# A fused attention and FFN kernel: batch 0's values loaded in three pieces, another order of the first FFN units, and two pieces of work moved behind batch 2's keys by values

## The chip, the cores and the metric

The kernel runs on one core of a Trainium2 chip. The metric is the device time of one execution in microseconds (us). The kernel before took 326.3 us (median of 3 runs, 325.94 to 326.5). All runs quoted here were in the same, fast state. A ratio is the mean time of one kernel's fast runs over the mean of the other's of the same rounds, so it is not quite the ratio of the medians beside it. Two or more kernels of one batch ran on the same chip and share the runs of the kernel before, so I compare within a batch first.

A profile comes from one execution. Differences of 0.1 to 1 us are below what one whole execution settles, but the profile prints starts to 0.01 us.

## The reference, cut to what matters

```python
q_p, k_p = phi(q), phi(k)             # relu times cos and relu times sin of the position
kv  = einsum('bhsf,bhsd->bhfd', k_p, v)   # per head: keys by values
z   = k_p.sum(axis=2)                     # taken along as a 65th column of v
x   = (q_p @ kv) / (q_p . z + 1e-6)   # 8 batches of 576 rows, 512 columns
g, val = x @ w_gate, x @ w_val        # FFN, 1536 columns in 12 column tiles
out = (gelu(g) * val) @ w_out         # float32, 4608 x 512
```

The inputs are q, k and v of 8 batches x 8 heads x 576 rows x 64. The attention is linear: after keys by values each row of q costs one small matmul and one division.

## The kernel before

All heavy work is on TensorE (PE). The program fixes the order of instructions on every engine by hand. The FFN works in blocks of 576 or 512 rows. Block 0 needs only batch 0's x. Each later block b carries batch b+1's attention between its units. A unit is a gate (four matmuls, then gelu on ScalarE, ACT) and a value (four matmuls, then a product on VectorE, DVE). There are eight PSUM banks, and each call names the bank it uses. To turn a tile is to transpose it by PE. The numerators of a tile are its small matmuls of q with keys by values, and dummies are matmuls without use that pass PE's time at the start.

```python
def gate(n, jt, c0, w, gb):            # 4 matmuls into bank gb, then gelu on ACT
    ...
    nc.scalar.activation(gel[:, 0:w], ps[:, gb, 0:w], AF.Gelu)
def value(n, jt, c0, w, vb):           # 4 matmuls into bank vb, then the product on DVE
    ...
    nc.vector.tensor_mul(hT..., gel[:, 0:w], ps[:, vb, 0:w])
def numer_mm(b, t, bank, g):           # group g of heads goes to bank + g: a tile uses TWO banks
    ... ps[0:rows, bank + g, ...]
def Y(t, bank):                        # numerators and division of x tile t of batch 0
    ...
def X(t, bank, eng):                   # x tile t turned by PE, copied to xT by eng
    ...
def q_by_pe(b, j, bank, eng):          # q tile j turned by PE, copied to qT by eng
    ...
```

The beginning of block 0 as the kernel before has it (cut):

```python
q_by_pe(0, 3, 6, "s")
gate(0, 2, *A, 5)                      # A: columns 0 to 255
X(2, 0, "v")()
sq(4, 1, "s"), sq(4, 0, "v")           # sine product of q tile 4 on ACT, cosine on DVE
gate(0, 3, *A, 4)
value(0, 2, *A, 7)
Y(3, 0)()
value(0, 3, *A, 2)
q_by_pe(0, 4, 3, "s")
gv_unit(0, 0, 256, 128, 5, 6)
gv_unit(0, 1, 256, 128, 4, 7, (X(3, 0, "s"),))
Y(4, 2)()
gv_unit(0, 0, 384, 128, 5, 1)          # "the unit at column 384"
```

The two later pieces that the change moves: `carry(0)`, a GpSimd (POOL) copy of 64 FFN columns from block 0's buffer to block 1's, and `attn_step(1, 5)`, the numerators and division of batch 1's last x tile (64 rows).

## Time and profile before

| view | value |
|---|---|
| median time, span of the profile | 326.3 us, 324.7 us |
| PE busy | 98% |
| first FFN gate | 16.63 us |
| turn of x tile 1 (four L343 after the first gates) | 17.21 us |
| unit at column 384 (L218) | 24.02 us |
| keys by values of batch 1, of batch 2 (L154) | 48.68, 67.55 us |

In a timeline row the columns are start, duration in us, engine, line, operation, what it writes and reads with shapes, the count of merged instructions and, in brackets, the idle time ahead of it with what ended it. A pipelined stream of four 128x512 matmuls is shown as 1.03 us long, but the next stream starts 0.86 us after it: I read starts, not ends. The lines themselves are in the prediction below.

### The profile page before, as it was taken

How to read it: one execution, taken by the hardware profiler on the slowest of the kernel's cores; microseconds unless marked ns; L12 is line 12 of the kernel's file. 1: busy time of each engine (PE TensorE's matmuls, PEld its weight loads, DVE VectorE, ACT ScalarE, POOL GpSimd, SP SyncE). 2: the span in 40 equal slices, each digit the busy share in tenths (PEclk: the TensorE clock that was granted, in tenths of full speed). 3: DMA queues.
4: the chain of work that ended last, by engine and by line, in shares of the span. 5: the costliest groups of instructions: out<-in, count | busy, mean ns of one | idle time of the engine just before them, and what ended most of it. 6: DMA issues, size and time to landing. Idle time of an engine off the chain costs nothing.

```text
span 324.7 us, 5863 instructions
## 1 busy us (share of the span) xinstructions
PE 317.4 (98%) x2218; PEld 167.3 (52%) x2218; DVE 168.2 (52%) x380; ACT 151.3 (47%) x271; POOL 22.0 (7%) x43
## 2 busy tenths in 40 slices
PE   7999999999999999999999999999999999999994
PEld 2597856455445544544455445544554444444443
DVE  5785776677663575366636574637454222222210
ACT  6574774852583247325642565237522222323321
POOL 2650010000100010001000100010000100100000
PEclk9999999999999999999999999999999999999999
DMA  7999999999999929991999279946433111000124
GB/s 228 284 204 275 232 295 311 333 217 155 299 193 356 206 50 194 324 245 51 191 324 239 55 147 299 302 66 121 107 70 78 32 32 34 32 32 32 37 63 97
DMA packets 88299, 55.56 MB, mean 171 GB/s; under 512 B 53072, under 2 KB 83536, under 8 KB 88272
## 3 DMA queue, kind: packets, MB, share of 16 engines
q1 hardware_dynamic: 81744, 48.84, 60.8%
q0 software_dynamic: 6096, 5.90, 10.2%
q10 hardware_dynamic: 432, 0.46, 0.5%
q8 instruction: 17, 0.28, 0.4%
q14 instruction: 10, 0.08, 0.1%
HBM read 37.75 MB, written 9.44 MB: 145 GB/s over the span
## 4 chain that ended last, share of the span: by engine, by line
PE 94%; DVE 3%; issue 1%; ACT 0%; DVEq 0%
PE ps L218 28%; PE ps L229 28%; PE ps L259 27%; PE ps L154 3%; PE ps L170 3%; PE ps L127 3%; DVE kp L135 1%; PE ps L324 1%; PE ps L277 1%; DVE vx L141 1%; PE ps L343 1%; DVE xb L185 0%; DVE rec L184 0%; ACT xT L346 0%; DVE qp L135 0%
## 5 line engine op out<-in xcount | busy, mean ns | idle before, releaser
L234 DVE TENSOR_TENSOR hT<-gel,ps 128x512 bf16<-128x512 f32 (+5 forms) x126 | 76.2, 608 | 92.1 <-PE ps L229 91.7
L218 PE MATMUL ps<-xT,wg_sb 128*128 128x512 bf16 (+5 forms) x504 | 113.4, 349 | 0.1
L229 PE MATMUL ps<-xT,wv_sb 128*128 128x512 bf16 (+5 forms) x504 | 113.2, 348 | 0.0
L223 ACT ACTIVATE gel<-ps 128x512 f32<-128x512 f32 (+5 forms) x126 | 67.4, 536 | 73.9 <-PE ps L218 48.8
L259 PE MATMUL ps<-wo_sb,hT 128*128 128x512 bf16 x420 | 96.5, 379 | 0.0
L218 PEld LDWEIGHTS <-wg_sb 128*128 128x128 bf16 x504 | 47.1, 98 | 44.5
L229 PEld LDWEIGHTS <-wv_sb 128*128 128x128 bf16 x504 | 45.7, 98 | 39.0
L259 PEld LDWEIGHTS <-hT 128*128 128x128 bf16 x420 | 40.8, 98 | 47.7
L288 ACT COPY o_sb<-ps 128x512 f32<-128x512 f32 x35 | 20.5, 586 | 76.0 <-PE ps L259 75.9
L185 DVE TENSOR_TENSOR xb<-ps,rec 128x512 bf16<-128x512 f32 (+2 forms) x41 | 27.8, 678 | 1.8 <-DMA xr<-xb 0.3
L182 DVE TENSOR_SCALAR den<-ps 128x8 f32<-128x8 f32 (+2 forms) x41 | 6.7, 164 | 41.1 <-PE ps L170 41.0
L137 ACT ACTIVATE kp<-kf,sin_c 128x512 bf16<-128x512 f32 (+1 forms) x41 | 25.4, 681 | 0.3 <-DMA kf<-in_k_dram 0.3
L170 PEld LDWEIGHTS <-qT 128*128 128x128 bf16 (+1 forms) x320 | 15.1, 98 | 8.3 <-issue 0.4
L137 ACT ACTIVATE qp<-qf,sin_c 128x512 bf16<-128x512 f32 x28 | 19.3, 714 | 0.0
L135 DVE TENSOR_SCALAR kp<-kf,cos_c 128x512 bf16<-128x512 f32 (+1 forms) x45 | 18.7, 463 | 0.8 <-DMA kf<-in_k_dram 0.8
L135 DVE TENSOR_SCALAR qp<-qf,cos_c 128x512 bf16<-128x512 f32 x40 | 17.8, 488 | 0.0
L170 PE MATMUL ps<-kv,qT 128*128 128x65 bf16 (+1 forms) x320 | 16.6, 194 | 0.1
L209 POOL COPY xT<-xr 128x256 bf16<-128x256 bf16 x7 | 2.8, 401 | 198.0 <-DMA xr<-xb 198.0
L127 PE MATMUL ps<-hT 128*128 128x512 bf16 x34 | 11.1, 484 | 1.7 <-DVE par_i L104 1.7
L154 PEld LDWEIGHTS <-kp 128*128 128x128 bf16 x320 | 10.8, 97 | 3.2 <-issue 0.9
L154 PE MATMUL ps<-vx,kp 128*128 128x65 bf16 x320 | 11.1, 193 | 0.6 <-DVE vx L141 0.3
L141 ACT CAST vx<-vf 128x1280 bf16<-128x1280 f32 (+1 forms) x9 | 9.7, 1076 | 1.2 <-DMA vf<-in_v_dram 1.2
(54 smaller groups left out, 89.0 us busy)
## 6 DMA issues: line engine op xcount, KB each, us to landing
out_dram<-o_sb SPq DMA_DIRECT2D x38, 128.0 KB, 2.4
kf<-in_k_dram SPq DMA_DIRECT2D x7, 640.0 KB, 7.1
out_dram<-o_sb SPq DMA_DIRECT2D x16, 256.0 KB, 2.8
qf<-in_q_dram SPq DMA_DIRECT2D x6, 640.0 KB, 5.9
vf<-in_v_dram SPq DMA_DIRECT2D x6, 640.0 KB, 8.8
kf<-in_k_dram SPq DMA_DIRECT2D x7, 512.0 KB, 6.0
qf<-in_q_dram SPq DMA_DIRECT2D x6, 512.0 KB, 4.9
vf<-in_v_dram SPq DMA_DIRECT2D x6, 512.0 KB, 7.8
```

Of the source, the lines that this page charges most:

```text
L127: nc.tensor.matmul(ps[:, bank, :], lhsT=junk[:, 0:128], rhs=junk, start=True, stop=True)
L135: nc.vector.tensor_scalar(d, s, col, 0.0, op0=ALU.mult, op1=ALU.max)
L137: nc.scalar.activation(d, s, AF.Relu, scale=col)
L154: nc.tensor.matmul(ps[:, bank, (h % 4) * (D + 1):(h % 4 + 1) * (D + 1)], lhsT=kp[:, j, h, :], rhs=vx[b % 2][:, j, h, 0:D + 1], start=(j == ...
L170: nc.tensor.matmul(ps[0:rows, bank + g, (h % 4) * (D + 1):(h % 4 + 1) * (D + 1)], lhsT=qT[b % 2][:, t, h, 0:rows], rhs=kv[b % 2][:, h, 0:D ...
L185: nc.vector.tensor_tensor(xb[0:rows, g0:g1], nd[:, :, :, 0:D], rec[0:rows, 0:n, :, None].to_broadcast([rows, n, 4, D]), op=ALU.mult,)
L218: nc.tensor.matmul(ps[:, gb, 0:w], lhsT=wg_sb[:, ct, jt * 128:(jt + 1) * 128], rhs=xT[:, ct, p0:p0 + w], start=(ct == 0), stop=(ct == CT - 1),
L223: nc.scalar.activation(gel[:, 0:w], ps[:, gb, 0:w], AF.Gelu)
L229: nc.tensor.matmul(ps[:, vb, 0:w], lhsT=wv_sb[:, ct, jt * 128:(jt + 1) * 128], rhs=xT[:, ct, p0:p0 + w], start=(ct == 0), stop=(ct == CT - 1),
L234: nc.vector.tensor_mul(hT[n % 2][:, jt, 64 + c0:64 + c0 + w], gel[:, 0:w], ps[:, vb, 0:w])
L259: nc.tensor.matmul(ps[:, bank, :], lhsT=hT[n % 2][:, jt, c0:c0 + 128], rhs=wo_sb[:, jt, :], start=(jt == 0), stop=(jt == JT - 1),)
L288: nc.scalar.copy(o_sb, ps[:, bank, :])
```

## The change

Its intent, as far as the code tells: start keys by values of batch 0 earlier by loading the second half of v in two pieces and by giving ACT and DVE other shares of the copies; drop four of the 34 dummy matmuls; put another FFN unit ahead of x tile 3's numerators; and take a POOL copy and a division out of the way of the keys by values of batches 1 and 2.

```diff
-    load(vf, v, 0, 4, 8)
+    load(vf, v, 0, 4, 6)
+    load(vf, v, 0, 6, 8)
 ...
-    kv_half(0, 0, 4, None)
-    q_evac(0, 1, 1, "v")
-    dummies(2)
+    kv_heads(0, 0, 4, 4)
+    q_evac(0, 0, 0, "v")
+    q_evac(0, 1, 1, "s", 0, 4)
     cast_v(0, 4, 6, "v")
-    cast_v(0, 6, 8, "s")
-    kv_evac(0, 0, 4, "v")
-    kv_half(0, 1, 5, "s")
+    cast_v(0, 6, 7, "v")
+    kv_evac(0, 0, 4, "s")
+    cast_v(0, 7, 8, "s")
+    dummies(1)
+    kv_heads(0, 4, 6, 5)
 ...                                    # numerators, second half of kv, q tile 2's turn moved
     q_by_pe(0, 3, 6, "s")
+    X(2, 0, "v")()
     gate(0, 2, *A, 5)
-    X(2, 0, "v")()
+    gate(0, 3, *A, 4)
     sq(4, 1, "s"), sq(4, 0, "v")
-    gate(0, 3, *A, 4)
+    gv_unit(0, 0, 256, 128, 1, 2)
+    Y(3, 0)()
     value(0, 2, *A, 7)
-    Y(3, 0)()
-    value(0, 3, *A, 2)
-    q_by_pe(0, 4, 3, "s")
-    gv_unit(0, 0, 256, 128, 5, 6)
-    gv_unit(0, 1, 256, 128, 4, 7, (X(3, 0, "s"),))
-    Y(4, 2)()
+    value(0, 3, *A, 3)
+    q_by_pe(0, 4, 6, "s")
+    gv_unit(0, 1, 256, 128, 5, 2, (X(3, 0, "s"),))
+    Y(4, 3)()
     gv_unit(0, 0, 384, 128, 5, 1)
 ...                                    # other banks for the units after it
-        (11, 1): (L(carry, 0), ),
 ...
-    mid[1][3].append(L(attn_step, 1, 5))
+    mid[1][5].append(L(attn_step, 1, 5, 4))
+    mid[1][5].append(L(carry, 0))
```

More of the change, by code (lines that the diff above doesn't have):

```diff
@@ L148, in turn_q, with kv_heads @@
         )
-    def kv_half(b, g, bank, eng="s"):
-        for h in range(4 * g, 4 * g + 4):
+    def kv_heads(b, h0, h1, bank):
+        for h in range(h0, h1):
             for j in range(NJ + 1):
@@ L159, in kv_half @@
                 )
-        if eng is not None:
-            kv_evac(b, g, bank, eng)
+    def kv_half(b, g, bank, eng="s"):
+        kv_heads(b, 4 * g, 4 * g + 4, bank)
+        kv_evac(b, g, bank, eng)
     def kv_evac(b, g, bank, eng):
@@ L363 @@
     load_w(4, 8)
-    for j in range(2):
-        sq(j, 0, "v"), sq(j, 1, "s")
-        q_by_pe(0, j, j, None)
-    dummies(3)
-    q_evac(0, 0, 0, "v")
+    sq(0, 0, "v"), sq(1, 1, "s"), sq(0, 1, "v"), sq(1, 0, "v")
+    q_by_pe(0, 0, 0, None)
+    q_by_pe(0, 1, 1, None)
+    dummies(2)
     cast_v(0, 0, 2, "v")
     cast_v(0, 2, 4, "s")
-    kv_half(0, 0, 4, None)
-    q_evac(0, 1, 1, "v")
-    dummies(2)
+    kv_heads(0, 0, 4, 4)
+    q_evac(0, 0, 0, "v")
+    q_evac(0, 1, 1, "s", 0, 4)
     cast_v(0, 4, 6, "v")
-    cast_v(0, 6, 8, "s")
-    kv_evac(0, 0, 4, "v")
-    kv_half(0, 1, 5, "s")
+    cast_v(0, 6, 7, "v")
[3 more added lines that the diff above has]
+    kv_heads(0, 4, 6, 5)
     x0, x1 = new_xb(), new_xb()
@@ L380 @@
     norm(x0, 6, 0, 1)
-    dummies(1, 4)
+    kv_heads(0, 6, 8, 5)
+    kv_evac(0, 1, 5, "s")
+    q_evac(0, 1, 1, "s", 4, 8)
+    dummies(1, 3)
     numer_mm(0, 0, 6, 1)
-    sq(2, 1, "s")
     norm(x0, 6, 1, 2)
-    sq(2, 0, "v")
+    x_by_pe(0, 0, x0, 4, "s", 0, 2)
+    sq(2, 0, "v"), sq(2, 1, "v")
     numer_mm(0, 1, 0, 0)
@@ L388 @@
     norm(x1, 0, 0, 2)
-    x_by_pe(0, 0, x0, 4, "s", 0, 2)
-    dummies(2, 5)
     x_by_pe(0, 0, x0, 4, "s", 2, 4)
-    q_by_pe(0, 2, 3, None)
     nc.gpsimd.tensor_copy(tiny[0:1, 1:2], x0[0:1, 1, 3, D - 1:D])
@@ L410 @@
     gate(0, 1, 0, 128, 4)
+    q_by_pe(0, 2, 3, None)
     X(1, 2, "s")()
@@ L421 @@
     q_by_pe(0, 3, 6, "s")
+    X(2, 0, "v")()
     gate(0, 2, *A, 5)
-    X(2, 0, "v")()
+    gate(0, 3, *A, 4)
     sq(4, 1, "s"), sq(4, 0, "v")
-    gate(0, 3, *A, 4)
+    gv_unit(0, 0, 256, 128, 1, 2)
+    Y(3, 0)()
     value(0, 2, *A, 7)
-    Y(3, 0)()
-    value(0, 3, *A, 2)
-    q_by_pe(0, 4, 3, "s")
-    gv_unit(0, 0, 256, 128, 5, 6)
-    gv_unit(0, 1, 256, 128, 4, 7, (X(3, 0, "s"),))
-    Y(4, 2)()
+    value(0, 3, *A, 3)
+    q_by_pe(0, 4, 6, "s")
+    gv_unit(0, 1, 256, 128, 5, 2, (X(3, 0, "s"),))
+    Y(4, 3)()
     gv_unit(0, 0, 384, 128, 5, 1)
-    gv_unit(0, 1, 384, 128, 4, 0)
+    gv_unit(0, 1, 384, 128, 6, 2)
     gate(0, 4, *A, 5)
     X(4, 7, "v")()
-    gate(0, 5, *A, 4)
-    gv_unit(0, 2, *Bw, 2, 6)
-    gv_unit(0, 3, *Bw, 3, 7)
-    value(0, 4, *A, 1)
-    value(0, 5, *A, 2)
-    gv_unit(0, 0, 512, 64, 4, 6)
-    gv_unit(0, 1, 512, 64, 5, 7)
+    gate(0, 5, *A, 0)
+    gv_unit(0, 2, *Bw, 1, 6)
+    gv_unit(0, 3, *Bw, 2, 7)
+    value(0, 4, *A, 3)
+    value(0, 5, *A, 4)
+    gv_unit(0, 0, 512, 64, 5, 6)
+    gv_unit(0, 1, 512, 64, 1, 7)
     load_q(1, nc.gpsimd)
```

## The prediction

> **What bounds the kernel now.** I read the page's busy shares and its chain that ended last, then the waits of PE, then the timeline of each engine over 10 to 25 us, 44 to 50 us and 62 to 71 us, where the edits lie. First the page:
>
> ```profile
> span 324.7 us, 5863 instructions
> ...
> PE 317.4 (98%) x2218; PEld 167.3 (52%) x2218; DVE 168.2 (52%) x380; ACT 151.3 (47%) x271; POOL 22.0 (7%) x43
> ...
> PE 94%; DVE 3%; issue 1%; ACT 0%; DVEq 0%
> ```
>
> PE is busy for 98% of the span and the chain that ended last is PE for 94%. From the first gate at 16.6 us to the last output tile PE runs FFN matmuls back to back. So time can be won only where PE really waits, or runs dummies to pass the time: in the first 25 us, and at two short places later. The timeline of the first attention steps:
>
> ```profile
> 11.20 0.81 PE L127 MATMUL ps<-hT 128*128 128x512 bf16 x3
> 11.56 0.55 DVE L141 CAST vx<-vf 128x640 bf16<-128x640 f32 x1
> 12.16 0.76 PE L154 MATMUL ps<-vx,kp 128*128 128x65 bf16 x20 [0.15 <-DVE vx L141]
> 12.20 0.73 ACT L141 CAST vx<-vf 128x640 bf16<-128x640 f32 x1 [0.98 <-DMA vf<-in_v_dram]
> 13.22 0.76 PE L154 MATMUL ps<-vx,kp 128*128 128x65 bf16 x20
> 14.15 0.16 DVE L182 TENSOR_SCALAR den<-ps 128x4 f32<-128x4 f32 x1 [0.65 <-PE ps L170]
> 15.64 0.48 DVE L135 TENSOR_SCALAR qp<-qf,cos_c 128x512 bf16<-128x512 f32 x1
> 16.03 0.16 DVE L182 TENSOR_SCALAR den<-ps 128x8 f32<-128x8 f32 x1
> 16.46 0.69 DVE L185 TENSOR_TENSOR xb<-ps,rec 128x512 bf16<-128x512 f32 x1
> 16.63 0.61 PE L218 MATMUL ps<-xT,wg_sb 128*128 128x128 bf16 x8
> 17.21 0.40 PE L343 MATMUL ps<-ident,xb 128*128 128x128 bf16 x4
> ```
>
> L127 is a dummy, L154 keys by values, L182 to L185 the division, L343 the turning of x. DVE is the serial resource here: the second x tile is ready at 16.46 + 0.69 = 17.15 and PE turns it at 17.21. The two later places, keys by values of batch 1 and of batch 2, with what stood before them:
>
> ```profile
> 45.13 2.63 DVE L135 TENSOR_SCALAR kp<-kf,cos_c 128x512 bf16<-128x512 f32 x5
> 45.27 1.01 POOL L245 COPY hT<-hT 128x768 bf16<-128x768 bf16 x1 [9.52 <-DVE hT L234]
> 48.68 1.36 PE L154 MATMUL ps<-vx,kp 128*128 128x65 bf16 x40 [0.18 <-DVE vx L141]
> ...
> 66.29 1.03 PE L229 MATMUL ps<-xT,wv_sb 128*128 128x512 bf16 x4
> 66.80 0.69 DVE L185 TENSOR_TENSOR xb<-ps,rec 128x512 bf16<-128x512 f32 x1
> 67.55 1.37 PE L154 MATMUL ps<-vx,kp 128*128 128x65 bf16 x40 [0.23 <-DVE xb L185]
> ```
>
> The stated 0.18 and 0.23 are short by the modelled drain: a stream of four such matmuls starts every 0.864 us though its row says 1.03. The second could have started at 66.29 + 0.86 = 67.15, so PE lost 0.40. The first follows 18 matmuls that began at 44.45, 18 x 0.216 = 3.89, so it could have started at 48.34 and lost 0.34.
>
> **What the Trainium skill says.** "SBUF — State Buffer", section "SBUF: two separate sides", says that VectorE and GpSimd share one port pair under an exclusive lock that a VectorE instruction in a 2-port mode and a GpSimd instruction take in turns. The trace agrees: the five kp instructions beside the POOL copy take 2.63, while at 64.32 three take 1.27 (0.42 each, so 2.1 for five): 0.5 lost. "TensorE: Matmul & The Clock Gate", Part 1 ("The HAM clock gate"), says that PE falls to half clock after an idle window of about 3.4 us. The longest wait here is about 0.5 us, so taking four dummies out should cost no clock; the trace shows granted clock 1.00 throughout. "ScalarE: Activation LUTs", section "What ACT_TABLE_LOAD costs", gives 186 ns + 0.833 ns per element for an instruction with immediate scale and bias; the trace's 640-element cast of 726 ns fits, so one head (320 elements) is an estimate of 0.45 us.
>
> **Part 1, the head (v by 4, 2, 2; other first units).** By the order of instructions, four dummies go (34 to 30). ACT takes over the copy of kv's first half and q's second tile in two halves; DVE takes over two sine products of q. Working forward with the old trace's durations:
> - PE ends the 16 turns of q near 11.20. Two dummies (0.43) instead of three, and the cast of heads 0-1 no longer behind the q copy: keys by values start at 11.63 instead of 12.16.
> - Their results are there 0.80 later, 12.43; ACT copies to 12.83; numerator at 12.88 (was 13.82); division starts at 13.21 (was 14.15), 0.94 early.
> - Values of heads 6-7 still land near 12.1 (before, ACT's cast waited for them to 12.20). Head 7's cast waits behind ACT's kv copy: 12.83 + 0.45 = 13.28. So keys by values end near 13.65, the second kv copy at 14.05, the second numerator at 14.10, its division starts at 14.43 (was 14.90) and ends at 15.26 (was 15.72): 0.46 early.
> - Now DVE does two products (15.24 to 16.12) where it did one (15.64 to 16.03), so the division of the second tile starts near 16.1 and is ready near 17.2: 17.15 before. The gain of 0.46 is spent on the 0.44 of the product moved from ACT.
> - The first gates can start near 16.06 instead of 16.63, but the eight turns of q tile 2 (0.45), which before filled the wait ahead of the gates, now stand behind them. The turn of x tile 1 comes at about 17.2 in both.
>
> From there PE is dense, and only the order of units counts. The pair that ends it is the copy of x tile 3 ahead of the unit at column 384: before, turning q tile 4 was followed by two units, so that ACT's copies of q (0.59), of gelu and of x (0.58) hid in part, and the unit at 24.02 had waited 0.26. Now one unit is put ahead of that turn: q tile 4 turned by 22.76, ACT: copy to 23.55, gelu to 23.75, x copy to 24.33, unit at 24.38. That is 0.36 later for the same work. Sum for the head: from 0 to +0.36, taken as **+0.3**, with an uncertainty of about 0.6 either way, as it is a chain of some fifteen steps each good to 0.05 to 0.1.
>
> **Part 2, the copy of FFN columns.** It leaves the stretch of kp products: DVE ends 0.5 earlier, the first cast of v at 48.2 instead of 48.63, before PE comes at 48.34. ACT's last sine product still ends at 47.73 + 0.72 = 48.45, needed by PE's fifth matmul (48.34 + 4 x 0.034 = 48.48). So nearly the whole 0.34 is won: **-0.3**. The copy itself runs near 77 us on POOL, where DVE's instructions read PSUM and PE has slack of about 2 us per value bank.
>
> **Part 3, batch 1's last tile.** Its numerator (0.25 of PE, unchanged) goes behind keys by values of batch 2, into bank 4. These no longer wait for the division to leave bank 6. PE would come at 66.9; heads 0-3 are cast at 66.46 (DVE), heads 4-7 at 67.04 (ACT), needed only 0.62 after the start. So the whole 0.40 is won: **-0.4**. The division and turn of that tile come later, but its tokens are in block 2, which starts near 88. DVE then has 1.1 + 0.69 = 1.8 us for each unit of 1.98 us of PE; it keeps up.
>
> Sum: +0.3 - 0.3 - 0.4 = -0.4.
>
> **The rivals.** First, the head gains what its first numerator suggests, up to 0.9. For: the new order starts real work earlier and has four dummies fewer. Against: DVE's chain to the second x tile, and DMA landings from the trace: the first gate weights land at 9.3 + 6.0 = 15.3, the first value weights at 16.6, the second pair at 19.25 and 20.4; gates of columns 2 began at 19.62, only 0.37 later. A head that runs 0.9 faster meets these, though the new order puts a turn of x ahead of that gate, which gives back 0.22. It would make 325.0. Second, the split load gives a new wait: one more pair of issues at about 0.62 each lets the last values land late and q's rest 1.3 later. The queue holds over 5 us of outstanding transfers (issue to landing 5.3 to 5.9), so issue is not what limits; if it were, numerators and the gates behind them slip by 0.5 to 0.8: 326.6. Third, the moved tile makes DVE or the transposing DMA late and PE waits for a value bank or a bank of numerators near 70 to 78, giving the 0.4 back: 326.2. The slack of 2 us speaks against it. Fourth, all is hidden: 326.3.
>
> **Range and chances.** Parts 2 and 3 are read directly from a wait and are likely (together -0.4 to -0.8); the head's sign is open (-0.7 to +0.7). I put the median of the time at 326.3 - 0.5 = 325.8, a tenth below the sum because a head reworked with trace in hand more likely won something, and the range at 325.0 to 326.6; runs of before alone spread over 0.56. A change over 2% is 6.5 us, more than all of PE's waits after the first matmul, so within 2% has 0.98.
>
> **What would show it.** Keys by values of batch 0 start near 11.6 and the first division near 13.2; the turn of x tile 1 stays near 17.2; the unit at column 384 starts at 24.0 to 24.4. Five kp products near 45 us take 2.1 to 2.2, and keys by values of batch 1 and 2 follow the matmuls before them without a wait. Wrong would be: the first gate unit starting at 16.1 with the x turn near 16.5 (the head wins), a wait on DMA at the value casts, or PE waits near 70 to 78 us.

## The result, and the profile after

The changed kernel took 327.25 us (median of 4, 326.98 to 327.51) against 326.25 for the kernel before: ratio 1.0031, 95% interval 1.0013 to 1.0048. It is slower by 1.0 us, within 2% as a class, but outside the predicted range of 325.0 to 326.6.

The page of the changed kernel, then its chain by line, of which the first and the last count here:

```profile
span 325.7 us, 5821 instructions
...
PE 314.2 (96%) x2181; PEld 167.0 (51%) x2214; DVE 168.2 (52%) x381; ACT 150.8 (46%) x272; POOL 22.0 (7%) x43
...
PE 91%; DVE 2%; DMA 2%; ACT 1%; issue 1%; SPq 1%; POOL 0%; DVEq 0%; POOLq 0%; ACTq 0%
```

PE's share of the chain falls from 94% to 91%, and ACT and a DMA are now in it. (The page lists 2181 matmuls but 2214 weight loads, so some matmul records are missing, and the busy sum of PE itself is no measure.) The waits of PE by line, total us, number and longest:

```profile
PE ps L173 <- ACT gel L226: 0.7, 1, 0.7
PE ps L327 <- DVE qp L136: 0.6, 1, 0.6
PE ps L221 <- ACT xT L349: 0.6, 2, 0.3
```

The first is new in kind: numerators (L173) that wait for a gelu (L226), which share no data. The timeline shows it, with the early stage above it:

```profile
11.01 0.73 ACT L142 CAST vx<-vf 128x640 bf16<-128x640 f32 x1 [0.86 <-DMA vf<-in_v_dram]
11.82 0.77 PE L155 MATMUL ps<-vx,kp 128*128 128x65 bf16 x20
13.66 0.16 DVE L185 TENSOR_SCALAR den<-ps 128x4 f32<-128x4 f32 x1 [0.29 <-PE ps L173]
17.43 0.40 PE L346 MATMUL ps<-ident,xb 128*128 128x128 bf16 x4
20.04 1.01 ACT L335 COPY qT<-ps 128x1024 bf16<-128x1024 bf16 x1 [0.62 <-PE ps L327]
20.95 0.67 ACT L226 ACTIVATE gel<-ps 128x256 f32<-128x256 f32 x2
21.46 0.29 PE L173 MATMUL ps<-kv,qT 128*128 128x65 bf16 x4
21.49 0.73 ACT L138 ACTIVATE qp<-qf,sin_c 128x512 bf16<-128x512 f32 x1
22.11 0.28 ACT L226 ACTIVATE gel<-ps 128x128 f32<-128x128 f32 x1
22.44 0.29 PE L173 MATMUL ps<-kv,qT 128*128 128x65 bf16 x4 [0.69 <-ACT gel L226]
25.38 0.38 PE L221 MATMUL ps<-xT,wg_sb 128*128 128x128 bf16 x4 [0.21 <-ACT xT L349]
```

In the kernel before the same eight numerators are one group, and the unit at column 384 is the last row:

```profile
21.15 0.42 PE L170 MATMUL ps<-kv,qT 128*128 128x65 bf16 x8
24.02 0.38 PE L218 MATMUL ps<-xT,wg_sb 128*128 128x128 bf16 x4
```

In the changed kernel they come in two halves, 0.98 us apart (21.46 and 22.44). Four numerators without a wait keep PE for 0.13 us (in the same trace four start at 13.34, and the next matmuls, keys by values, at 13.47): 0.85 lost. The second half writes bank 1, into which the inserted gate unit had written; its gelu reads bank 1, and ACT runs it last, after a 1.01 us copy of q, two gelus and a sine product. The last row of the changed kernel is the unit at column 384: 25.38 against 24.02, 1.36 later. Here are the two later places:

```profile
45.81 4.05 PE L262 MATMUL ps<-wo_sb,hT 128*128 128x512 bf16 x17
46.48 2.06 DVE L136 TENSOR_SCALAR kp<-kf,cos_c 128x512 bf16<-128x512 f32 x5
49.69 1.43 PE L155 MATMUL ps<-vx,kp 128*128 128x65 bf16 x40
...
67.11 1.03 PE L232 MATMUL ps<-xT,wv_sb 128*128 128x512 bf16 x4
67.98 1.37 PE L155 MATMUL ps<-vx,kp 128*128 128x65 bf16 x40
```

The five kp products take 2.06 (2.63 before). Keys by values of batch 1 start 3.88 after the output matmuls ahead of them (4.23 before), those of batch 2 start 0.87 after their stream (1.26 before). Both waits are gone, as intended.

The account of this profile: +1.36 by the unit at column 384, then -0.28 and -0.39, which leaves +0.69. DVE's last copy starts at 321.08 instead of 320.39, also +0.69. The other 0.3 of the span's +1.0 lies after that copy, where only the last output transfers are left.

### The profile page after: what moved, and what is told of

It is laid out like the page before. It is cut to its first block, busy times and chain, and to the rows that moved or that the text cites. A ratio compares the mean times of both kernels' runs of the same rounds, so it can differ in the third digit from the quotient of the medians.

```text
span 325.7 us, 5821 instructions
## 1 busy us (share of the span) xinstructions
PE 314.2 (96%) x2181; PEld 167.0 (51%) x2214; DVE 168.2 (52%) x381; ACT 150.8 (46%) x272; POOL 22.0 (7%) x43
## 4 chain that ended last, share of the span: by engine, by line
PE 91%; DVE 2%; DMA 2%; ACT 1%; issue 1%; SPq 1%; POOL 0%; DVEq 0%; POOLq 0%; ACTq 0%
PE ps L232 28%; PE ps L221 28%; PE ps L262 28%; PE ps L173 3%; PE ps L155 3%; DMA vf<-in_v_dram 2%; PE ps L280 1%; SPq L80 1%; PE ps L346 0%; DVE vx L142 0%; DVE xb L188 0%; PE ps L327 0%; ACT gel L226 0%; DVE qp L136 0%; ACT qT L335 0%
## 5 line engine op out<-in xcount | busy, mean ns | idle before, releaser
L221 PE MATMUL ps<-xT,wg_sb 128*128 128x512 bf16 (+5 forms) x492 | 111.6, 348 | 1.2 <-ACT xT L349 0.6
L232 PE MATMUL ps<-xT,wv_sb 128*128 128x512 bf16 (+5 forms) x496 | 111.6, 348 | 0.4
L226 ACT ACTIVATE gel<-ps 128x512 f32<-128x512 f32 (+5 forms) x126 | 67.3, 536 | 73.9 <-PE ps L221 52.0
L262 PE MATMUL ps<-wo_sb,hT 128*128 128x512 bf16 x408 | 94.3, 379 | 0.6
L173 PEld LDWEIGHTS <-qT 128*128 128x128 bf16 (+1 forms) x320 | 15.3, 98 | 9.3 <-issue 1.3
L138 ACT ACTIVATE qp<-qf,sin_c 128x512 bf16<-128x512 f32 x26 | 17.9, 714 | 0.0
L173 PE MATMUL ps<-kv,qT 128*128 128x65 bf16 (+1 forms) x320 | 17.0, 194 | 0.9 <-ACT gel L226 0.7
L128 PE MATMUL ps<-hT 128*128 128x512 bf16 x29 | 9.1, 476 | 1.7 <-DVE par_i L105 1.7
L142 ACT CAST vx<-vf 128x1280 bf16<-128x1280 f32 (+2 forms) x9 | 9.4, 1047 | 0.9 <-DMA vf<-in_v_dram 0.9
```

Source lines behind the costliest of these rows:

```text
L138: nc.scalar.activation(d, s, AF.Relu, scale=col)
L142: cp(vx[b % 2][:, :, h0:h1, 0:D], vf[:, h0:h1].rearrange("p h j d -> p j h d"))
L173: nc.tensor.matmul(ps[0:rows, bank + g, (h % 4) * (D + 1):(h % 4 + 1) * (D + 1)], lhsT=qT[b % 2][:, t, h, 0:rows], rhs=kv[b % 2][:, h, 0:D ...
L221: nc.tensor.matmul(ps[:, gb, 0:w], lhsT=wg_sb[:, ct, jt * 128:(jt + 1) * 128], rhs=xT[:, ct, p0:p0 + w], start=(ct == 0), stop=(ct == CT - 1),
L232: nc.tensor.matmul(ps[:, vb, 0:w], lhsT=wv_sb[:, ct, jt * 128:(jt + 1) * 128], rhs=xT[:, ct, p0:p0 + w], start=(ct == 0), stop=(ct == CT - 1),
L262: nc.tensor.matmul(ps[:, bank, :], lhsT=hT[n % 2][:, jt, c0:c0 + 128], rhs=wo_sb[:, jt, :], start=(jt == 0), stop=(jt == JT - 1),)
```

## The experiments

Twelve kernels ran, in three batches of four. I give each as an edit against the kernel before or the changed one. "The head" is what comes up to the unit at column 384, "the early stage" its part up to the turn of x tile 1. The table holds times of the profile in us. "v" is the start of ACT's first cast of v, which stands at the landing of v's first half. "turn" is the turn of x tile 1, "384" the unit at column 384.

| kernel | v | turn | turn - v | 384 | 384 - turn | median us | ratio to before |
|---|---|---|---|---|---|---|---|
| before | 10.50 | 17.21 | 6.71 | 24.02 | 6.81 | 326.25 | 1 |
| changed | 11.01 | 17.43 | 6.42 | 25.38 | 7.95 | 327.25 | 1.0031 |
| old_head | 10.62 | 16.99 | 6.37 | 23.81 | 6.82 | 325.78 | 0.9976 |
| head_alone | 10.64 | 16.96 | 6.32 | 24.91 | 7.95 | 327.53 | 1.0030 |
| bank | 10.65 | 17.04 | 6.39 | 24.48 | 7.44 | 326.75 | 1.0002 |
| sine_later | 10.79 | 17.14 | 6.35 | 24.49 | 7.35 | 326.85 | 1.0009 |
| after_again | 10.57 | 16.96 | 6.39 | 24.90 | 7.94 | 326.81 | 1.0015 |
| old_units | 10.79 | 17.11 | 6.32 | 23.95 | 6.84 | 325.45 | 0.9974 |
| bank_sine | 10.37 | 16.71 | 6.34 | 23.81 | 7.10 | 326.16 | 0.9995 |
| v_whole | 10.87 | 17.57 | 6.70 | 25.52 | 7.95 | 327.36 | 1.0032 |
| copy_alone | 10.69 | 17.40 | 6.71 | 24.21 | 6.81 | 326.24 | 0.9993 |
| tile_alone | 10.46 | 16.84 | 6.38 | 23.65 | 6.81 | 326.00 | 0.9985 |
| late_v_old | 12.21 | 18.87 | 6.66 | 25.68 | 6.81 | 327.30 | 1.0020 |
| late_v_new | 11.66 | 18.07 | 6.41 | 24.88 | 6.81 | 326.48 | 1.0001 |

The kernel before had medians of 326.61, 326.30 and 326.45 in the three batches. The column "384 - turn" is the cleanest measure: it repeats to 0.03 between kernels with the same order of units, wherever the stretch begins.

### Batch 1: which part loses

My theory was that the head loses 1.36 us, that the two late moves win 0.28 and 0.39, and that the parts add. The rival was that the late moves are paid for later, or that the loss was a chance late landing.

**old_head**: the kernel before with the late moves alone.

```diff
-        (11, 1): (L(carry, 0), ),
-    mid[1][3].append(L(attn_step, 1, 5))
+    mid[1][5].append(L(attn_step, 1, 5, 4))
+    mid[1][5].append(L(carry, 0))
```

> The first 44 us as in the kernel before, with the late tile and the late copy of the changed kernel. My theory: the changed kernel loses 1.36 us in its head (unit at column 384 at 25.38 instead of 24.02) and wins 0.28 at keys by values of batch 1 and 0.39 at those of batch 2; the parts add. So here 0.67 less than before: near 325.6 us, ratio 0.998, with the unit at column 384 at 24.0, keys by values of batch 1 near 48.35 and the unit after those of batch 2 about 0.4 earlier than the 0.28 alone gives. Rival: the two late moves cost something later that the trace of the changed kernel hides (xb's buffers, POOL), so about 326.3 as before.

It measured 325.78 us against 326.61, ratio 0.9976 (0.9963 to 0.9989): 0.8 us less, a little more than the 0.67 expected; in the profiled run the turn of x tile 1 also came 0.22 earlier. Keys by values of batch 1 start 3.89 after the output matmuls (48.12 and 44.23), those of batch 2 0.86 after their stream. A part is paid back on the spot: the 40 matmuls of batch 1 take longer than in the changed kernel (1.43) or before (1.36).

```profile
48.12 1.56 PE L154 MATMUL ps<-vx,kp 128*128 128x65 bf16 x40
```

ACT's sine products of batch 1 had waited 0.39 for the landing of k, so the last of them ended at 48.37, after PE needed it. So the copy's move won 0.14 here and not 0.28, and DVE's last copy stands at 319.64, 0.75 earlier than before (0.22 + 0.14 + 0.39). No other wait of PE is listed after 24 us. It beats both the kernel before and the changed one.

**head_alone**: the changed kernel with the late moves undone.

```diff
-    mid[1][5].append(L(attn_step, 1, 5, 4))
-    mid[1][5].append(L(carry, 0))
+    mid[1][3].append(L(attn_step, 1, 5))
+        (11, 1): (L(carry, 0), ),
```

> The head of the changed kernel with the tile and the copy where the kernel before has them. Theory: 1.36 more than before, near 327.6 us, unit at column 384 at 25.4, and both later waits back (0.34 and 0.40 ahead of keys by values of batch 1 and 2). Rival: the head is only 0.3 slower by its order and the rest of 1.36 was a late landing of k and v in that execution: near 326.6.

It measured 327.53 against 326.61, 1.0030 (1.0018 to 1.0042): 0.9 more, where theory said 1.36 and the rival 0.3. The trace says why it lies between: v landed at 10.6, not 11.0, so the turn came 0.25 earlier than before, but the stretch from the turn to column 384 took 7.95 as in the changed kernel, 1.14 more than before. So 1.14 of the loss belongs to the order of units, and the remaining 0.22 of the 1.36 was the landing of v in that execution. The two later waits are back (4.22 and 1.25).

**bank**: the changed kernel, the inserted gate in bank 3.

```diff
-    gv_unit(0, 0, 256, 128, 1, 2)
+    gv_unit(0, 0, 256, 128, 3, 2)
-    value(0, 3, *A, 3)
-    q_by_pe(0, 4, 6, "s")
+    value(0, 3, *A, 6)
+    q_by_pe(0, 4, 3, "s")
```

> The changed kernel with the inserted gate unit in bank 3 instead of bank 1 (and the value after it in bank 6, the turn of q tile 4 in bank 3), so that the numerators of tile 3, which use banks 0 and 1, don't wait for its gelu. Theory: PE's wait of 0.69 ahead of the second half of these numerators goes. If the bank is the whole cause, the time falls by 0.8 to 0.9 against the changed kernel (326.4). My finer count: the gelu stays last in ACT's queue, DVE's product that needs it stands ahead of the division of tile 3, so the turn of x tile 3 waits till about 23.9 and the unit at column 384 comes at about 25.0: only 0.35 less (326.9), the wait moved from the bank to ACT's queue.

326.75 us, 1.0002 of before. The wait of 0.69 is gone and the eight numerators run as one group, yet the stretch fell only from 7.95 to 7.44. So 0.51 of the removed 0.85 was won, and 0.34 became a wait further on, as the finer count had it (it expected 0.35 won):

```profile
21.06 0.42 PE L173 MATMUL ps<-kv,qT 128*128 128x65 bf16 x8
22.64 0.39 PE L221 MATMUL ps<-xT,wg_sb 128*128 128x128 bf16 x4
23.41 0.40 PE L346 MATMUL ps<-ident,xb 128*128 128x128 bf16 x4 [0.38 <-DVE xb L188]
```

The turn of x tile 3 (L346) waits for its division. DVE must first do the product of the inserted unit, and that waits for the same late gelu. So the shared bank was one way in which ACT's queue reached PE, and not the only one.

**sine_later**: the changed kernel, bank 1 kept, ACT's sine product one place later.

```diff
-    sq(4, 1, "s"), sq(4, 0, "v")
+    sq(4, 0, "v")
     gv_unit(0, 0, 256, 128, 1, 2)
+    sq(4, 1, "s")
```

> The changed kernel with ACT's sine product of q tile 4 behind the gelu of the inserted gate unit instead of ahead of it, bank 1 kept. If ACT's queue is the cause, that gelu ends at about 21.85 instead of 22.40, the numerators of tile 3 wait about 0.15 instead of 0.69, and the unit at column 384 comes at about 24.9: 0.5 less than the changed kernel (326.75). If only the bank counts and the queue does not, less than 0.1.

326.85 us, 1.0009; the stretch took 7.35, 0.60 less. The order of ACT's queue is thus a cause: nothing else was changed. It isn't the whole, as bank 1 still makes the second half wait a little: the numerators are one group with a gap inside (0.67 instead of 0.42 long).

The row totals of this batch have wide spreads (head_alone 327.01 to 328.28, sine_later 326.27 to 327.83) while old_head stayed within 325.69 to 326.07. I therefore rest the verdict on the stretch and not on these medians.

### Batch 2: the head taken apart

**after_again**: the changed kernel with a comment added.

> The changed kernel again, as the measure for its variants in the same rounds. In the first batch kernels with the old head spread over 0.4 to 0.6 us and those with the new head over 1.3 to 1.6. Theory: the time of a new head follows the landing of v (casts right at the landing), so ratio to before 1.001 to 1.003 with a spread of over 1 us; from the turn of x tile 1 to the unit at column 384 it takes 7.95 us again, whatever v did.

326.81 against 326.30, ratio 1.0015 (1.0002 to 1.0028), with 7.94 for the stretch. So the changed kernel is slower on repetition, but by half of the first figure: in this profile v landed at 10.57 instead of 11.01. My expected spread of over 1 us was wrong; it was 0.8.

**old_units**: the changed kernel up to q tile 3, then the order and banks of the kernel before.

```diff
     q_by_pe(0, 3, 6, "s")
-    X(2, 0, "v")()
     gate(0, 2, *A, 5)
+    X(2, 0, "v")()
     ...                                # and so on: the listing of the kernel before
```

> The changed kernel up to the turn of q tile 3, the units of block 0 after it in the order and banks of the kernel before, both late moves kept. Theory: all of the loss is in the order of units, so the turn of x tile 1 to the unit at column 384 takes 6.8 as before instead of 7.95, and the time is 1.1 less than the changed kernel's and within 0.3 of the old head with the late moves (ratio to before 0.9975). Rival: part of the loss lies in the early stage (v by 4, 2, 2): then it stays 0.3 or more above that.

325.45 us, 0.9974 (0.9962 to 0.9987): 1.36 less than after_again. The stretch is 6.84, as before. This is the fastest of all runs, level with old_head (0.9976). All of the loss is in the order of units after q tile 3; the early stage with v by 4, 2, 2 costs nothing, and by the ratios it wins nothing over the old one either.

**bank_sine**: both edits of batch 1 together.

```diff
-    sq(4, 1, "s"), sq(4, 0, "v")
-    gv_unit(0, 0, 256, 128, 1, 2)
+    sq(4, 0, "v")
+    gv_unit(0, 0, 256, 128, 3, 2)
+    sq(4, 1, "s")
-    value(0, 3, *A, 3)
-    q_by_pe(0, 4, 6, "s")
+    value(0, 3, *A, 6)
+    q_by_pe(0, 4, 3, "s")
```

> The changed kernel with both the bank of the inserted unit and the place of ACT's sine product altered. Alone they took the stretch from the turn of x tile 1 to the unit at column 384 from 7.95 to 7.44 and 7.35. If they act on one and the same wait, both give about 7.3; if the queue of ACT holds what is left after the bank, 7.15 (0.8 less than the changed kernel). Not below 6.8 in any case: what is left is ACT's q copy, gelu and x copy right ahead of the unit.

326.16 us, 0.9995. The stretch took 7.10, against the expected 7.15: of the 1.14 lost, 0.85 came back, which is just the gap between the two halves of the numerators. What is left, 7.10 - 6.81 = 0.29, is the tail of the stretch:

```profile
21.86 0.61 PE L327 MATMUL ps<-ident,qp 128*128 128x128 bf16 x8
22.51 0.59 ACT L337 COPY qT<-ps 128x512 bf16<-128x512 bf16 x1 [0.84 <-PE ps L327]
23.00 0.28 ACT L226 ACTIVATE gel<-ps 128x128 f32<-128x128 f32 x1
23.16 0.59 ACT L349 COPY xT<-ps 128x512 bf16<-128x512 bf16 x1
23.81 0.38 PE L221 MATMUL ps<-xT,wg_sb 128*128 128x128 bf16 x4 [0.21 <-ACT xT L349]
```

ACT has a copy, a gelu and a copy to do between the turn of q tile 4 and the unit at column 384, and PE has one unit less to run meanwhile than before. This is read from the trace; no run varies it alone.

**v_whole**: the changed kernel with the second half of v loaded whole.

```diff
-    load(vf, v, 0, 4, 6)
-    load(vf, v, 0, 6, 8)
+    load(vf, v, 0, 4, 8)
```

> The changed kernel with the second half of v loaded whole as before (two transfers instead of four). If the split is what made k and v land late in the profiled execution of the changed kernel (k 0.5, v 0.4 later), they land at about 7.1 and 10.5 here and the time falls by 0.3 or more. If that was chance, k and v land as in the other runs, casts of heads 4-6 start about 0.1 to 0.3 later, and the time is within 0.2 of the changed kernel's.

327.36 us, 1.0032, so 0.55 slower than after_again: I had expected less than 0.2. From the landing to the turn it takes 6.70 instead of 6.39, because DVE's cast of heads 4 to 6 now waits for the whole half (0.51 idle until 12.56, where after_again casts at 11.66). So the split earns 0.3 in this head. In the profiled run v also landed 0.3 later (10.87); together that is the 0.63 by which DVE's last copy is later than in after_again (321.23 and 320.60). That the split made v late in the changed kernel finds no support: without the split v landed no earlier, in the one execution profiled.

### Batch 3: the late moves one by one, and a late v

**copy_alone**: only `carry(0)` moved.

```diff
-        (11, 1): (L(carry, 0), ),
+    mid[1][5].append(L(carry, 0))
```

> The kernel before with nothing but the copy of FFN columns moved behind batch 2's keys by values. Theory: the five kp products near 45 us take 2.1 instead of 2.63, keys by values of batch 1 start 3.89 after the output matmuls ahead of them began instead of 4.23, and their own 40 take 0.05 to 0.1 longer, as the last sine product ends later than they reach it: 0.28 less, ratio 0.9991. The wait ahead of batch 2's keys by values stays (0.40). Rival: the copy's time is given back where it now stands, ratio 1.000.

326.24 against 326.45, 0.9993 (0.9981 to 1.0006), which by itself is no clear result. The trace is clear: kp products in 2.06, keys by values of batch 1 3.88 after the output matmuls, the wait of batch 2 kept (1.25).

```profile
44.64 4.05 PE L259 MATMUL ps<-wo_sb,hT 128*128 128x512 bf16 x17
45.31 2.06 DVE L135 TENSOR_SCALAR kp<-kf,cos_c 128x512 bf16<-128x512 f32 x5
48.52 1.43 PE L154 MATMUL ps<-vx,kp 128*128 128x65 bf16 x40
```

**tile_alone**: only batch 1's last tile moved.

```diff
-    mid[1][3].append(L(attn_step, 1, 5))
+    mid[1][5].append(L(attn_step, 1, 5, 4))
```

> The kernel before with nothing but batch 1's last tile moved. Theory: keys by values of batch 2 start 0.864 after the stream ahead of them instead of 1.26: 0.39 less, ratio 0.9988, and the five kp products near 45 us still take 2.6. With copy_alone the two sum to what old_head won (0.0024).

326.00 us, 0.9985 (0.9972 to 0.9997). Batch 2's keys by values start 0.86 after their stream, and the kp products still take 2.63. The two savings sum to 0.0022, against 0.0024 for both at once.

**late_v_old** and **late_v_new**: old_head and old_units with one needless 128 KB transfer ahead of v.

```diff
+    spare = rot.tile([128, 512], FP32, name="gel", bufs=4)
+    nc.sync.dma_start(out=spare[0:64]..., in_=k[0, 0:2]...)
     load(vf, v, 0, 0, 4)
```

> The old head with the two late moves, with one needless transfer of 128 KB ahead of v, so that v lands about 0.4 to 0.6 later. Question: does the landing of v set the head in both kernels or in the new one alone? In the old head the second half's cast stood right at its landing (12.31), so I expect the turn of x tile 1 to shift by nearly the whole delay. Rival: the old head has slack (its first cast began 0.49 after the landing) and the turn shifts by less than 0.2.

> The same needless transfer in the new early stage with the old order of units (old_units). The casts of the first half stand at their landing, so the turn of x tile 1 comes 6.3 to 6.4 after that landing as in the other new heads, later by the whole delay; the time against old_units by 0.4 to 0.6 more (ratio to before 0.999).

v's first half landed 1.59 later in the old head and 0.87 later in the new one; I had meant 0.4 to 0.6 in both, and the runs don't say why the same transfer cost so unlike amounts. Nor did v move alone: q, ahead of it in the queue, landed 1.03 and 0.44 later too. The question can still be answered: the turn came 1.88 later in the old head (18.87 against 16.99) and 0.96 later in the new one (18.07 against 17.11), and in both the stretch after it kept 6.81. In both the casts of v start at its landing (in the old head DVE waited 0.55 for the second half, in the new one 0.81 for the first). So a landing of v this late sets the turn in either head, and most of it passes to the end: DVE's last copy is 1.74 and 0.75 later. That agrees with the excess of the first measurement over the second, but only one of the changed kernel's four first executions was profiled, so that v was late in the others is argued, not shown.

## Why the prediction was right or wrong

**Wrong: the head.** I put it at +0.3. The step that failed is "From there PE is dense, and only the order of units counts." I had followed PE's and DVE's queues through the inserted unit, but not the bank that its gate uses against the second bank of the numerators behind it, nor ACT's queue ahead of its gelu. Both are in the code: the numerators of tile 3 are given bank 0 and use bank 0 and 1, the inserted gate is given bank 1, and ACT has a 1.01 us copy, two gelus and a sine product first. The Trainium skill states in "TensorE: Matmul & The Clock Gate", Part 1 ("The HAM clock gate"), that "ACT/DVE are strict FIFO"; the trace agrees, as PE was at the value behind that gate by 21.24 and the gate's gelu started at 22.11. That term measured 0.85 us (0.98 - 0.13), and bank_sine gave it back. Moving the bank alone gave back 0.51 and moving the sine product alone 0.60, so both belong to it.

**Right: the x copy ahead of column 384.** I put it at +0.36. With the other term removed, 0.29 was left.

**Mis-sized: the early stage.** I had the first division at 13.2 and the turn of x tile 1 at 17.2 "in both", a gain of nothing. The first division came at 13.66 in the changed kernel with v 0.5 late, and at 13.19 in after_again; the turn at 17.43 and 16.96. From the landing of v to the turn it takes 6.3 to 6.4 in the new head and 6.71 in the kernel before, so against that execution it gains about 0.3. Yet in old_head and tile_alone the old order also took 6.37 and 6.38. The rows that differ are these of the dummies (PE's weight loads; the first fence is the kernel before, the second tile_alone):

```profile
7.26 0.15 PEld L127 LDWEIGHTS <-hT 128*128 128x128 bf16 x1 [0.28 <-issue]
7.69 0.34 PEld L127 LDWEIGHTS <-hT 128*128 128x128 bf16 x2 [0.28 <-issue]
```

```profile
5.99 0.15 PEld L127 LDWEIGHTS <-hT 128*128 128x128 bf16 x1 [0.28 <-issue]
6.41 0.53 PEld L127 LDWEIGHTS <-hT 128*128 128x128 bf16 x3 [0.27 <-issue]
```

The dummies are 0.43 apart at first and 0.21 later. The switch comes near 7.7 in one execution and near 6.4 in the other, so the turns of q, which stand behind the 26 dummies, start at 10.30 or at 9.66. In the old order DVE's cast of v stands behind its copy of the turned q, so late turns delay it (11.56 against 10.93); in the new order the cast stands ahead, and old_units, whose switch also came at 7.69, took 6.32. I read one execution as if it were the kernel. (That the clock stood at "1.00 throughout" shows nothing about the dummies left out: the same view says 1.00 while these dummies run at the slow distance.)

**Right: part 2 and part 3.** I put them at -0.3 and -0.4. By the traces of the changed kernel and of copy_alone and tile_alone they are 0.28 and 0.39, and old_head won 0.8 us of time. The margin of 0.03 that I gave ACT's last sine product was too thin, though: in old_head and old_units these products waited 0.39 and 0.48 for batch 1's k, keys by values took 1.56 and 1.65, and only 0.14 and 0.05 of the 0.28 were won.

**The rivals.** The first (the head wins up to 0.9) did not occur. Of the second, the sign that I named was there: in the changed kernel the first casts of v waited for the DMA, ACT 0.86 and DVE 0.23. But the extra issue isn't what costs: v_whole, without it, is the slower one. The third did not occur; DVE waited 0.92 for an x buffer (0.31 before), and PE had no wait near 70 to 78 us.

**The sum.** With the terms as measured against the profile of before: early stage -0.25 (after_again's turn at 16.96 against 17.21), bank and queue +0.85, x copy +0.29, late moves -0.67, together +0.22. after_again's last DVE copy starts at 320.60 against 320.39: +0.21. Its median of +0.5 has 0.3 more, of which the profile shows only that the span after that copy is 0.1 longer; the rest is not explained, and lies within the spread of its runs (0.8). My 325.8 was short by 0.85 for the missed term, which is nearly the distance to the second measurement (326.81); the first, 327.25, had v's late landing besides, in its profiled run.

## What to carry to other kernels

When a unit is put ahead of another, list for each engine what stands in its queue before the unit's last step, and for each bank who must have read it before the next write; a gelu late in one queue can hold up matmuls that share no data with it. Removing such a wait at the bank alone shifts a part of it to the next user of the same late result (0.34 of 0.85 us here), so look for the late producer too. A stage that comes earlier can meet the next late transfer, as keys by values of batch 1 met the landing of k in old_head. And where a change has parts, run them apart: here the two late moves alone (0.9976) beat the whole change (1.0015 to 1.0031).

## What the Trainium skill lacked or had wrong

- "TensorE: Matmul & The Clock Gate", Part 1, puts the end of the slow phase at around 4 us of sustained activity, give or take 0.5. Here the dummies began at 1.74 and ran at the slow distance until 5.99 (after_again), 6.41 (tile_alone) or 7.69 (before), so 4.3 to 6.0 us, with the same 26 dummies. The page also calls the point run-variable, as its window runs freely, and counts 6, 11 or 14 slow matmuls for one kernel. The 10 to 14 slow dummies here (4.3 to 6.0 us at 0.43 apart) fit that count, but the 1.7 us between these executions does not fit half a microsecond. The profile's granted clock says 1.00 for that time.
- "SBUF — State Buffer", section "SBUF: two separate sides", says that the loser of the shared ports is fully blocked. The 1.01 us POOL copy cost DVE's five products 0.57 in all (2.63 against 2.06), and the copy itself took 0.82 where it now stands beside DVE work that reads PSUM. The page gives no such case to size the loss from.
- No page says how far the landing of equal transfers varies: with the same k, q and first v transfers at the head of the queue, ACT's first cast of v began at 10.37 to 11.01 us in the twelve kernels without the extra transfer, and where v was made later still, most of it passed to the end of this kernel (1.74 and 0.75 us at DVE's last copy, for 1.59 and 0.87 at v).
